# Loading v two tokens to a partition and putting it into key blocks with 0/1 matrices on TensorE

## The chip, the cores and the metric

The kernel runs on one core of a Trainium2 chip. The metric is the device time of one execution in microseconds (us). In the runs that compared the two kernels, the kernel before had a median of 204.88 us over four runs, 203.87 to 207.5. Medians are taken over all runs of a kernel, slow ones too. Ratios are the mean time of one kernel's fast runs over the mean of the other's fast runs of the same rounds, so they are not quite the ratios of the medians quoted. "Fast" and "slow" name two states that executions fall into: a run more than 1.5% above the fastest of its kernel in the same rounds is called slow, as the 207.5 us is.

## The reference, cut to what matters

```python
# q, k, v: [4, 8, 768, 64] float32; heads 0, 2, 6 are "retrieval" heads, the others "stream" heads
scores = q @ k.T / 8                      # causal; stream heads keep 4 sink tokens and a window of 64
a = softmax(scores)
attn = a @ v                              # -> x: [3072 tokens, 512]
# then a mixture of 8 experts, one expert for each token, tokens with x @ w_skip <= 0 skipped
y = gate * (relu(x @ w1[e]) @ w2[e]);  out = x + y
```

The change touches only how v reaches the product `a @ v`, and when some row buffers are zeroed for the expert layers.

## The kernel before

The attention loop works on 16 pairs of heads. Pass i computes the scores of pair i in chunks of 1,024 columns (two PSUM buffers, `pst`), takes their exp on ScalarE into `at`, and does the weighing, `at` times v, of pair i-1. It also transposes q and k of pair i+1. v is used from `va`, a buffer of six key blocks of 128 tokens with one token to a partition and a column of ones for the sum of the softmax. For stream heads there is also a shifted copy `vx`, in which the sink tokens are put into each block. Two `va` and two `vx` buffers alternate.

```python
vv = v.rearrange("b h (n p) d -> b p h n d", p=P)      # a run of memory is 64 floats, 256 B
...
def cast_v(i):
    va, vx = vab[i % 2], vxb[i % 2]
    nc.gpsimd.tensor_copy(va[:, :, :, :D], v32[i])      # float32 -> float16, straight into key blocks
    if i:
        nc.scalar.activation(xgs[i], xgs[0], ACT.Copy)  # zero one row buffer
    for hi, hh in enumerate(heads(i)[1]):
        if not IS_RETR[hh]:
            nc.gpsimd.tensor_copy(vx[:, hi], va[:, hi, :NQB - 1])
            nc.gpsimd.tensor_copy(vx[:N_SINK, hi], va[:N_SINK, hi, 0:1].to_broadcast(...))
...
for i in range(NPR + 2):                    # one pass
    cast_v(i); load_qk(i + 3); load_v(i + 2)
    step(0); transpose(i + 1, "q"); step(1)             # step: scores and exp of one chunk
    weigh(i - 1, 0)
    step(2); transpose(i + 1, "k"); cast_qk(i + 2)
    # some passes: gate_weight, left  (routing work on VectorE)
    step(3); gate_transpose(i - 2); weigh(i - 1, 1); step(4)
    # some passes: place, right       (routing work)
    gate_logits(i - 2)
```

GpSimd and VectorE run their instructions in the order in which they were written. In the kernel before, for example, one `gx` starts on GpSimd at 110.76 us though its numerators were done at 104.32, behind a cast that waited 10.09 us for v and the copies after it; and VectorE takes up sums at 60.95 us that TensorE had finished at 59.12, behind an operation of 2.15 us.

The softmax here doesn't subtract the row's maximum and nothing guards it: scores larger than these inputs give would overflow.

## Time and profile before

| | before |
|---|---|
| time, median | 204.88 us |
| profiled span, TensorE clock | 201.9 us, 0.958 |
| TensorE busy | 163.2 us, 81% |
| ordinary pass of the loop | 6.05 us |
| last exp of the gate (end of attention, start of the last routing) | 121.28 us |

Two waits of TensorE matter. In the list of waits the columns are: who waited and for whom, us in total, how often, the longest.

```profile
PE pst L578 <- ACT at L606: 9.3, 14, 0.8
PE opsa L626 <- POOL va L505: 4.0, 1, 4.0
```

The first is the regular wait for a score buffer, about 0.7 us in a pass: it is slack that TensorE has after the second chunk. The second is the one wait for v, of pair 14, near the end of the loop; behind it, from 109.82 to 113.59 us, the granted clock was 0.55. A good measure is the start of ScalarE's copy `qT` of each pair: the difference of two neighbours is the length of one pass.

### The profile page before, as it was taken

The numbers are of one execution on the slowest core, as the hardware profiler recorded it, in microseconds if no ns is written. First come the engines' busy times: TensorE is split into PE (matmuls) and PEld (weight loads), VectorE is DVE, ScalarE is ACT, GpSimd is POOL, SyncE is SP. The second block draws the span as 40 slices with busy tenths as digits, with TensorE's granted clock in tenths as the row PEclk, the third lists the DMA queues.
The fourth block names the chain that finished last, engine by engine and source line by source line (L and its number), as shares of the span: only waits on it lengthen the run. The fifth ranks groups of instructions, "written<-read, shape, count | busy, mean of one in ns | idle before, by whom it ended". The sixth has DMA issues, their size and how long they took to land.

```text
span 201.9 us, 4741 instructions
## 1 busy us (share of the span) xinstructions
PE 163.2 (81%) x1896; PEld 119.3 (59%) x1896; DVE 109.5 (54%) x254; ACT 113.0 (56%) x164; POOL 119.3 (59%) x179
## 2 busy tenths in 40 slices
PE   0487999889888898888982757978999999999920
PEld 0366666676666676666852443378678678665700
DVE  5323666636899668997650678253444534534020
ACT  5998888897688977888891420035143144130400
POOL 7585499687387693788403901687858575133311
PEclk9999999999999999999998795999999999999985
DMA  5999699999899999999999899479999999999501
GB/s 173 295 345 287 169 174 238 316 327 318 236 245 201 301 343 296 342 266 214 215 275 232 204 234 174 103 181 246 232 239 233 239 245 233 235 245 248 165 14 63
DMA packets 47856, 47.12 MB, mean 233 GB/s; under 512 B 28484, under 2 KB 43588, under 8 KB 46802
## 3 DMA queue, kind: packets, MB, share of 16 engines
q0 software_dynamic: 6976, 21.56, 50.3%
q1 hardware_dynamic: 40850, 25.17, 44.3%
q8 instruction: 17, 0.28, 0.6%
q14 instruction: 13, 0.11, 0.2%
HBM read 56.64 MB, written 10.49 MB: 333 GB/s over the span
## 4 chain that ended last, share of the span: by engine, by line
ACT 27%; DMA 26%; PE 23%; issue 8%; DVE 7%; POOL 6%; POOLq 1%; SPq 0%; ACTq 0%; DVEq 0%
ACT at L606 15%; DMA out_dram<-xg,idx_s 14%; DMA vf<-in_v_dram 10%; PE pst L578 5%; ACT xg L507 4%; PE pst L588 4%; PE hps L971 4%; ACT qT L526 4%; ACT gxT L675 3%; PE opsa L626 3%; POOL out_dram L1001 2%; PE pst L595 2%; PE yps L991 2%; POOL xg L935 2%; DMA xg<-out_dram,idx_s 1%
## 5 line engine op out<-in xcount | busy, mean ns | idle before, releaser
L606 ACT ACTIVATE at<-pst 128x1024 f16<-128x1024 f32 (+2 forms) x76 | 61.3, 836 | 17.2 <-PE pst L600 13.3
L978 ACT ACTIVATE ht<-hps 128x512 f16<-128x512 f32 x32 | 19.1, 598 | 49.4 <-PE hps L971 49.4
L588 PE MATMUL pst<-qT,kz 128*128 128x128 f16 (+2 forms) x288 | 35.8, 242 | 2.5 <-ACT qT L526 2.1
L588 PEld LDWEIGHTS <-kz 128*128 128x128 f16 x288 | 24.1, 100 | 21.9 <-issue 12.8
L535 DVE COPY kz<-tps 64x768 f16<-64x768 f16 x28 | 26.6, 950 | 9.7 <-PE tps L518 9.3
L971 PE MATMUL hps<-xT,w 128*128 128x256 f16 x256 | 29.2, 273 | 1.2 <-DVE xT L961 1.2
L971 PEld LDWEIGHTS <-w 128*128 128x128 f16 x256 | 27.9, 113 | 2.8 <-issue 1.5
L578 PE MATMUL pst<-smask,ident 128*128 128x512 f16 (+1 forms) x60 | 22.3, 372 | 8.7 <-ACT at L606 8.7
L991 PE MATMUL yps<-w,ht 128*128 128x512 f16 x128 | 28.8, 379 | 0.0
L1001 POOL DMA_INDIRECT out_dram<-xg,idx_s x16 | 16.4, 1022 | 18.5 <-issue 8.5
L649 POOL CAST gx<-xh 128x768 f16<-128x768 f32 x15 | 12.4, 828 | 19.3 <-DVE xh L641 14.5
L999 DVE SCALAR_TENSOR_TENSOR xg<-yps,gsl,xg 128x512 f32<-128x512 f32 x16 | 12.0, 750 | 20.4 <-PE yps L991 20.3
L626 PE MATMUL opsa<-va,at 128*128 128x65 f16 x372 | 19.8, 196 | 4.0 <-POOL va L505 4.0
L935 POOL DMA_INDIRECT xg<-out_dram,idx_s x16 | 16.8, 1047 | 8.6 <-issue 4.3
L626 PEld LDWEIGHTS <-at 128*128 128x128 f16 x472 | 17.9, 99 | 5.4 <-issue 4.2
L505 POOL CAST va<-vf 128x768 f16<-128x768 f32 x16 | 14.0, 876 | 11.2 <-DMA vf<-in_v_dram 11.1
L637 DVE RECIPROCAL rec<-opsa 128x6 f32<-128x6 f32 x32 | 6.2, 194 | 26.3 <-PE opsa L626 25.9
L991 PEld LDWEIGHTS <-ht 128*128 128x128 f16 x128 | 12.3, 98 | 13.5
L641 DVE TENSOR_TENSOR xh<-opsa,rec 128x384 f32<-128x384 f32 x32 | 17.8, 556 | 1.3
L499 POOL CAST qin<-qf 128x768 f16<-128x768 f32 x16 | 13.1, 818 | 3.3 <-DMA qf<-in_q_dram 3.3
L499 POOL CAST kin<-kf 128x768 f16<-128x768 f32 x16 | 13.1, 822 | 1.0 <-DMA kf<-in_k_dram 0.8
L518 PE MATMUL tps<-ident,qin 128*128 128x128 f16 x96 | 8.7, 231 | 5.9 <-POOL qin L499 5.9
(117 smaller groups left out, 260.7 us busy)
## 6 DMA issues: line engine op xcount, KB each, us to landing
w<-in_moe_w_dram POOLq DMA_DIRECT2D x14, 1024.0 KB, 10.7
qf<-in_q_dram SPq DMA_DIRECT2D x16, 384.0 KB, 6.3
kf<-in_k_dram SPq DMA_DIRECT2D x16, 384.0 KB, 6.0
vf<-in_v_dram SPq DMA_DIRECT2D x32, 192.0 KB, 6.0
out_dram<-xh SPq DMA_DIRECT2D x7, 768.0 KB, 6.8
w<-in_moe_w_dram POOLq DMA_DIRECT2D x4, 512.0 KB, 12.4
out_dram<-xh SPq DMA_DIRECT2D x2, 384.0 KB, 5.2
xg<-out_dram,idx_s POOLq DMA_INDIRECT x16, 7.2
```

The lines of the kernel that those rows point to most:

```text
L499: nc.gpsimd.tensor_copy(h16, qk32[name, i].rearrange("p h n d -> p n h d"))
L535: nc.vector.tensor_copy(to, ti[r])
L578: nc.tensor.matmul(pst[:, bank - c0:bank - c0 + mw], C.ident, rmask.unsqueeze(1).to_broadcast([P, mw // P, P]) if retr else smask[:, bank: ...
L588: nc.tensor.matmul(pst[:, cols], kz[:, j * P:(j + 1) * P], qT[i][:, qb * P:(qb + n) * P], start=mw <= 0, stop=mw <= 0 or last)
L606: nc.scalar.activation(ats[i][:, b0:b0 + cn], pst[:, :cn], ACT.Exp, scale=SCALE)
L626: nc.tensor.matmul(opsa[:, qb, :], ats[i][:, b0 + c:b0 + c + P], vb, start=(n == 0), stop=(n == len(plan) - 1))
L641: nc.vector.tensor_mul(xhs[i // 2][:, :, 2 * (i % 2) + hi, :], opsa[:, :, :D], rec.to_broadcast([P, NQB, D]))
L935: ins = nc.gpsimd.indirect_dma_start(out=xgs[t], out_offset=None, in_=out[:, :], in_offset=bass.IndirectOffsetOnAxis(ap=idx_s[:, t:t + 1], ...
L971: nc.tensor.matmul(hps[:, fi, :], wts[e, 0][:, s].rearrange("p (t c r) -> p t r c", c=P, r=WR)[:, fs // WR, fs % WR], xTs[e][:, s, :], sta ...
L978: nc.scalar.activation(ht[:, 2 * f2:2 * f2 + 2], hps, ACT.Relu)
L991: nc.tensor.matmul(ypss[s2], hts[e][:, fs, s2 * P:(s2 + 1) * P], wts[e, 1][:, fs, :], start=(fs == 0), stop=(fs == FS - 1))
L1001: ins = nc.gpsimd.indirect_dma_start(out=out[:, :], out_offset=bass.IndirectOffsetOnAxis(ap=idx_s[:, t:t + 1], axis=0), in_=xgs[t], in_off ...
```

## The change

The intent: v in runs of 512 B halves the number of its packets (q1 28,562 in all, instead of 40,850). Two tokens then lie side by side on a partition, which is not the order that the key blocks need, so four matmuls with 0/1 matrices (`pick`) bring them into place through PSUM. In return, eleven of the fifteen zeroings move to the routing.

```diff
-    vv = v.rearrange("b h (n p) d -> b p h n d", p=P)
+    vv = v.rearrange("b h (m p n) d -> b p h m (n d)", p=P, n=2)
...
-  tr_ps bufs=2, ov_ps bufs=2          # PSUM: transposes, sums of attention
+  tr_ps bufs=3, ov_ps bufs=1
...
+        pick = ac_pool.tile([P, 2, 2, P], FP16, name="pick")      # zeros, then:
+                nc.vector.tensor_copy(pick[:, half, n, n::2], C.ident[:, half * D:(half + 1) * D])
...
         def cast_v(i):
-            nc.gpsimd.tensor_copy(va[:, :, :, :D], v32[i])
-            if i:
-                nc.scalar.activation(xgs[i], xgs[0], ACT.Copy)
+            v16[i] = qk_in_pool.tile([P, 2, NQB // 2, 2, D], FP16, tag="vin", name="vin")
+            nc.gpsimd.tensor_copy(v16[i]..., v32[i])
+            zero(i)                                  # passes 3, 7, 11, 15 only
+        def order_v(i):
+            for half in range(2):
+                vps = tr_psum.tile([P, 2, NQB // 2, D], FP32, tag="tps", name="vps")
+                for n in range(2):
+                    nc.tensor.matmul(vps, pick[:, half, n], v16[i][:, :, :, n], start=n == 0, stop=n == 1)
+                to = va[:, :, half::2, :D]
+                if half == 0:
+                    nc.scalar.activation(to, vps, ACT.Copy)
+                else:
+                    nc.vector.tensor_copy(to, vps)
+            shift_v(i)                               # the two GpSimd copies into vx, as before
...
                 # end of the pass, behind place and right:
+                if i < NPR:
+                    order_v(i)
...
+            for t in range(5, NT):                   # in the routing, after the loop
+                nc.scalar.activation(xgs[t], xgs[0], ACT.Copy)
```

(The last pair's second head also takes its PSUM tile from the score buffers; the cut leaves that out.)

More of the change, by code (lines that the diff above doesn't have):

```diff
@@ L415 @@
          tc.tile_pool(name="st_ps", bufs=2, space=bass.MemoryType.PSUM) as st_psum, \
-         tc.tile_pool(name="tr_ps", bufs=2, space=bass.MemoryType.PSUM) as tr_psum, \
+         tc.tile_pool(name="tr_ps", bufs=3, space=bass.MemoryType.PSUM) as tr_psum, \
          tc.tile_pool(name="at", bufs=2) as at_pool, \
-         tc.tile_pool(name="ov_ps", bufs=2, space=bass.MemoryType.PSUM) as ov_psum, \
+         tc.tile_pool(name="ov_ps", bufs=1, space=bass.MemoryType.PSUM) as ov_psum, \
          tc.tile_pool(name="oo", bufs=3) as o_pool, \
@@ L438 @@
         nc.vector.memset(xgs[0], 0.0)
+        pick = ac_pool.tile([P, 2, 2, P], FP16, name="pick")
+        nc.vector.memset(pick, 0.0)
+        for half in range(2):
+            for n in range(2):
+                nc.vector.tensor_copy(
+                    pick[:, half, n, n::2],
+                    C.ident[:, half * D:(half + 1) * D])
         NPR = B * H // 2
-        qk32, v32, qk16, qT, ats, xhs, x16s, xTs = ({} for _ in range(8))
+        qk32, v32, v16, qk16, qT, ats, xhs, x16s, xTs = ({} for _ in range(9))
         gpss = {}
@@ L489, in load_v @@
             b, hs = heads(i)
-            vf = ld_pool.tile([P, 2, NQB, D], FP32, tag="vf", name="vf")
+            vf = ld_pool.tile([P, 2, NQB // 2, 2 * D], FP32, tag="vf",
+                              name="vf")
             for hi, hh in enumerate(hs):
@@ L503, in cast_v, with zero, shift_v @@
         def cast_v(i):
-            va, vx = vab[i % 2], vxb[i % 2]
-            nc.gpsimd.tensor_copy(va[:, :, :, :D], v32[i])
-            if i:
-                nc.scalar.activation(xgs[i], xgs[0], ACT.Copy)
+            v16[i] = qk_in_pool.tile([P, 2, NQB // 2, 2, D], FP16, tag="vin",
+                                     name="vin")
+            nc.gpsimd.tensor_copy(
+                v16[i].rearrange("p h m n d -> p h m (n d)"), v32[i])
+            zero(i)
+        def order_v(i):
+            va, vx = vab[i % 2], vxb[i % 2]
+            for half in range(2):
+                vps = tr_psum.tile([P, 2, NQB // 2, D], FP32, tag="tps",
+                                   name="vps")
+                for n in range(2):
+                    nc.tensor.matmul(vps, pick[:, half, n],
+                                     v16[i][:, :, :, n], start=n == 0,
+                                     stop=n == 1)
+                to = va[:, :, half::2, :D]
[4 more added lines that the diff above has]
+            shift_v(i)
+        def zero(i):
+            if i % 4 == 3:
+                nc.scalar.activation(xgs[(i + 1) // 4], xgs[0], ACT.Copy)
+        def shift_v(i):
+            va, vx = vab[i % 2], vxb[i % 2]
             for hi, hh in enumerate(heads(i)[1]):
@@ L622, in weigh @@
                                      vx[:, hi, qb - 1]))
-            opsa = ov_psum.tile([P, NQB, D + 1], FP32, tag="opsa",
-                                name="opsa")
+            if i == NPR - 1 and hi == 1:
+                last_ps = st_psum.tile([P, CH], FP32, tag="pst", name="opsl")
+                opsa = last_ps[:, :NQB * (D + 1)].rearrange(
+                    "p (n d) -> p n d", n=NQB)
+            else:
+                opsa = ov_psum.tile([P, NQB, D + 1], FP32, tag="opsa",
+                                    name="opsa")
             for n, (qb, c, vb) in enumerate(plan):
```

## The prediction

> **What bounds the kernel now.** I read the page first, then the timeline engine by engine for one ordinary pass of the attention loop and for its end, then the DMA issues. The kernel has an attention loop over 16 pairs of heads (to about 115 us), a routing stretch (to 132 us) and the expert layers (to 193 us).
>
> ```profile
> PE 163.2 (81%) x1896; PEld 119.3 (59%) x1896; DVE 109.5 (54%) x254; ACT 113.0 (56%) x164; POOL 119.3 (59%) x179
> ...
> q0 software_dynamic: 6976, 21.56, 50.3%
> q1 hardware_dynamic: 40850, 25.17, 44.3%
> ```
>
> DMA looks nearly full throughout, but v's landing time (a median of 6.0 us in the list of DMA issues) is far shorter than the prefetch distance of v (two passes, 12 us), so for most of the loop nobody waits for it. The timeline of an ordinary pass shows who does (ScalarE, then TensorE):
>
> ```profile
> 58.36 1.02 ACT L606 ACTIVATE at<-pst 128x1024 f16<-128x1024 f32 x1 [0.66 <-PE pst L600]
> 59.28 0.80 ACT L675 ACTIVATE gxT<-xtp 128x768 f16<-128x768 f16 x1
> 59.97 1.57 ACT L606 ACTIVATE at<-pst 128x384 f16<-128x384 f32 x2
> 61.44 0.81 ACT L526 ACTIVATE qT<-tps 128x768 f16<-128x768 f16 x1
> 62.13 1.63 ACT L606 ACTIVATE at<-pst 128x1024 f16<-128x1024 f32 x2
> 64.41 1.02 ACT L606 ACTIVATE at<-pst 128x1024 f16<-128x1024 f32 x1 [0.66 <-PE pst L600]
> ```
> ```profile
> 60.04 0.38 PE L588 MATMUL pst<-qT,kz 128*128 128x128 f16 x3
> ...
> 63.21 0.38 PE L578 MATMUL pst<-smask,ident 128*128 128x512 f16 x1 [0.74 <-ACT at L606]
> ```
>
> The period is 64.41 - 58.36 = 6.05 us. ScalarE idles 0.66 us in it, TensorE 0.74 us, both at the same place: with two score buffers, TensorE fills the fourth chunk (1.2 us) only when the second chunk's exp has freed its buffer. Everywhere else the two alternate. One point matters: the next pass's first chunk leaves TensorE at 60.42 us (60.04 + 0.38) and its exp starts at about 60.5, so there the slack is 0.1 us.
>
> Near the end a transfer does bind:
>
> ```profile
> 98.29 0.56 POOL L382 DMA_DIRECT2D w<-in_moe_w_dram  x1
> 108.94 0.83 POOL L505 CAST va<-vf 128x768 f16<-128x768 f32 x1 [10.09 <-DMA vf<-in_v_dram]
> ```
> ```profile
> 105.51 0.28 PE L595 MATMUL pst<-qT,kz 128*64 128x128 f16 x2
> 109.82 1.26 PE L626 MATMUL opsa<-va,at 128*128 128x65 f16 x21 [4.03 <-POOL va L505]
> ```
>
> v of pair 14 lands late: the queue issuing it was blocked for 10.47 us while 1 MB weight loads went out. TensorE stands for 4.03 us and then runs slowly: from 109.82 to 113.59 it does work that takes 2.4 us elsewhere, some 1.35 us more. So v's small transfers cost about 5.4 us, in this one place.
>
> [...] v now goes in runs of 64 floats, 256 B: 32 x 768 = 24,576 of the 40,850 packets of q1[...]. [...] (from 90 to 109 us q0 held 78% and q1 24%). [...] the trace's 512-column matmul at 57.16 us is followed at 57.37, 0.21 us[...]. [...] the trace has 492 ns for that exp, about 0.42 us net where instructions overlap.
>
> **The change part by part.**
>
> Loads: two tokens to a partition make runs of 512 B, 12,288 packets instead of 24,576. In the late stretch q1 had to pass one output store (768 packets) and v of pair 14 (1,536); now 768 + 768, two thirds. v lands about 5 us earlier after issue, and each pass also gets longer. I expect the wait to go: -4.0 and -1.35 us.
>
> Zeroing: nothing. The built order of ScalarE is the same in both programs: ten of the fifteen zero copies first, then qT, four more, and one in the first pass. The scheduler hoists the eleven copies written in the routing, because nothing holds them back. So the 8.1 us of these copies stay where they are, and ScalarE gets no relief in the loop.
>
> Reordering: 4 matmuls of 384 columns per pair, [...]0.65 us of TensorE, one ScalarE copy (0.42 us) and one VectorE copy (estimated 0.5 us, from 0.56 us for the 128x384 multiply from PSUM). They stand between the last chunk of a pass and the first chunk of the next, the place with 0.1 us of slack. The chunk leaves TensorE at 60.42 + 0.65 = 61.07, its exp begins 0.55 to 0.62 us later, and the rest of the period follows it. ScalarE's copy (60.5 to 60.9) fits before that. In the first two passes TensorE waits there anyway (0.1 us each); passes 2, 3, 4, 7, 8, 11, 12 and 14 pay about 0.62; passes 5, 9 and 13, where the gate logits already wait 0.25 us for ScalarE, about 0.45; passes 6 and 10 about 0.6. Sum 0.2 + 5.0 + 1.4 + 1.2 = 7.8 us.
>
> VectorE order: in the built order the VectorE half of the copy stands behind the routing work of its pass. In pass 7:
>
> ```profile
> 58.77 2.15 DVE L807 TENSOR_TENSOR Lall<-iota,posi 128x768 f16<-128x768 f16 x1
> 60.95 0.20 DVE L637 RECIPROCAL rec<-opsa 128x6 f32<-128x6 f32 x1
> 61.18 0.56 DVE L641 TENSOR_TENSOR xh<-opsa,rec 128x384 f32<-128x384 f32 x1
> 61.65 0.25 DVE L815 TENSOR_TENSOR oht<-iota,posi 128x96 f16<-128x96 f16 x1
> 61.93 1.10 DVE L819 TENSOR_TENSOR Rall<-oht,val 128x384 f16<-128x384 f16 x1
> 62.96 0.19 DVE L824 TENSOR_REDUCE ohn<-oh 128x8 f32<-128x48 f16 x1
> 63.18 0.56 DVE L825 TENSOR_TENSOR acc<-acc,ohn 128x8 f16<-128x8 f16 x1
> ```
>
> So va is whole at about 63.7 + 0.5 = 64.2 us, while TensorE wants it at 61.03 + 0.65 = 61.7: 2.5 us of wait, 0.74 of it slack, about 1.65 left. Pass 11 gives 1.35 by the same reckoning, passes 6 and 10 (behind the placing, then two GpSimd copies of 0.45 us) about 0.75 each: 4.5 us at most. The durations there depend on what GpSimd does at the time, so I count half, 2.2 us.
>
> Tail: the last pair's weighing now needs matmuls, evictions, the routing's VectorE work and GpSimd's shifted copies first: about 1.5 us.
>
> Buffers: the third transpose buffer removes a wait of 0.56 us in passes 6 and 10, but there v's first tile waits for VectorE's k copies, so I count none. The single output buffer is normally read out within 0.8 us, long before its next use.
>
> Sum: 7.8 + 2.2 + 1.5 - 5.4 = +6.1 us; 204.4 + 6.1 = 210.5 us.
>
> **The rivals.**
>
> A: DMA is the bound, and halving v's packets gives more than one wait back. For it: the DMA row at 9 nearly throughout. Against: before the end GpSimd waited for v only once, 1.0 us at 69 us, and nobody behind it stood still. It would give 196 to 201 us.
>
> B: the reordering hides in TensorE's and ScalarE's idle time. For it: both idle about 0.7 us a pass, as much as the change adds. Against: that idle time lies after the second chunk's exp, and the work is put before the first chunk. With it hidden only the wait removed and the tail count: about 200.5 us.
>
> C: every wait I found is real: all 4.5 us of VectorE order, 213 us. For it: the built order. Against: the pass gets longer too and VectorE, 54% busy, may catch up.
>
> D: the wait for v of pair 14 stays, because weights still hold the engines and the reordering needs v some 2 us earlier than the weighing did. The need is one end-of-pass later than the cast, though, and two longer passes lie between. It would add 3 to 5 us.
>
> **Range and chances.** C and my half of it span 210 to 213; B, or part of it, pulls towards 200 to 206, and whoever split the PSUM buffers so carefully may have seen a gain. I take 210.5 us with 203 to 215 for 8 in 10. The lines of 2% are 200.3 and 208.5: faster 0.10, same 0.30, slower 0.60.
>
> **What would show it.** Right: an ordinary pass of about 6.65 us instead of 6.05, with ScalarE waiting for TensorE before the first chunk's exp; the wait for v at pair 14 gone; TensorE waiting for va in the passes after 7 and 11; q1 with 28,562 packets; ScalarE still zeroing at the start. Wrong: a period still near 6.05 (then B), a shorter period everywhere (then A), or va's waits being absent, which takes the 2.2 us out.

## More of the kernel before

`weigh(i, 1)` ends with numerators on VectorE (`xh`) and a GpSimd copy for the gate (`gx`).

## The result, and the profile after

| | before | changed |
|---|---|---|
| time, median of four | 204.88 us | 214.8 us (213.56 to 216.28) |
| ratio of fast runs | | 1.0504, 95% interval 1.0407 to 1.0602 |
| profiled span, clock | 201.9 us, 0.958 | 212.1 us, 0.956 |
| ordinary pass | 6.05 us | 6.70 us |
| last exp of the gate | 121.28 us | 131.89 us |

The changed kernel is 5% slower. All of it is there by the end of attention: 131.89 - 121.28 = 10.6 us. From there to the end both kernels take about 80 us.

The queue row of the page (packets, MB, share of the engines' time) shows the load as intended, against 40,850 packets before:

```profile
q1 hardware_dynamic: 28562, 25.17, 37.7%
```

The ordinary pass on ScalarE (start, duration, engine, line, what; in brackets the idle time ahead of it and who ended it):

```profile
38.08 0.81 ACT L562 ACTIVATE qT<-tps 128x768 f16<-128x768 f16 x1
...
43.10 0.49 ACT L533 ACTIVATE va<-vps 128x384 f16<-128x384 f32 x1
43.86 1.02 ACT L642 ACTIVATE at<-pst 128x1024 f16<-128x1024 f32 x1 [0.28 <-PE pst L624]
44.78 0.81 ACT L562 ACTIVATE qT<-tps 128x768 f16<-128x768 f16 x1
```

The new copy `va<-vps` is there, and ScalarE now waits for TensorE right before the first chunk's exp. From `qT` to `qT` it is 6.70 us. In the passes with routing work TensorE also stands before the weighing:

```profile
60.44 0.19 PE L667 MATMUL opsa<-va,at 128*128 128x65 f16 x1 [1.15 <-DVE va L535]
61.54 0.19 PE L667 MATMUL opsa<-vx,at 128*128 128x65 f16 x1 [0.91 <-POOL vx L547]
...
62.42 0.38 PE L614 MATMUL pst<-smask,ident 128*128 128x512 f16 x1
```

First the VectorE half of the new copy is missing, then GpSimd's shifted copies. The list of waits sums them up; neither row was there before. Not all of these 10.3 us are lost, since part of them falls into slack that TensorE had anyway; experiment 6 measures what they cost:

```profile
PE opsa L667 <- DVE va L535: 6.8, 5, 1.6
...
PE opsa L667 <- POOL vx L547: 3.5, 4, 0.9
```

Near the end, GpSimd's cast of v of pair 14 waits for nothing any more. That of pair 15 still waits a little, and nobody behind it stands still for it:

```profile
111.75 0.82 POOL L517 CAST vin<-vf 128x768 f16<-128x768 f32 x1
120.79 1.60 POOL L517 CAST vin<-vf 128x768 f16<-128x768 f32 x1 [1.21 <-DMA vf<-in_v_dram]
```

And the last pair pays for the reordering once more:

```profile
125.38 0.21 PE L667 MATMUL opsa<-va,at 128*128 128x65 f16 x1 [1.59 <-DVE va L535]
126.49 0.22 PE L667 MATMUL opsa<-vx,at 128*128 128x65 f16 x1 [0.89 <-POOL vx L547]
```

**A side effect on VectorE.** In a routing pass one small operation grew. Before, and then in the changed kernel:

```profile
48.39 0.49 DVE L732 SCALAR_TENSOR_TENSOR eq<-sub,erev 128x48 f32<-128x48 f32 x1
```
```profile
51.25 2.65 DVE L773 SCALAR_TENSOR_TENSOR eq<-sub,erev 128x48 f32<-128x48 f32 x1
```

In the changed kernel GpSimd casts v, q and k back to back from 51.48 to 53.84 us, and the small operation ends just after them: 0.49 us became 2.65 us. (Even the 0.49 us stood beside a GpSimd copy; at 121.22 us in the kernel before, with no GpSimd cast or copy at that time, the operation took 0.21 us.) That the casts stretch it is what these three records suggest; no run here isolates it, or separates how much of the total it costs.

### The profile page after: what moved, and what is told of

The parts are those of the page before. It is cut to its first block, busy times and chain, and to the rows that moved or that the text cites. A ratio compares the mean times of both kernels' runs of the same rounds, so it can differ in the third digit from the quotient of the medians.

```text
span 212.1 us, 4981 instructions
## 1 busy us (share of the span) xinstructions
PE 174.3 (82%) x1960; PEld 125.7 (59%) x1960; DVE 120.5 (57%) x275; ACT 120.1 (57%) x180; POOL 119.5 (56%) x179
## 3 DMA queue, kind: packets, MB, share of 16 engines
q1 hardware_dynamic: 28562, 25.17, 37.7%
## 5 line engine op out<-in xcount | busy, mean ns | idle before, releaser
L624 PE MATMUL pst<-qT,kz 128*128 128x128 f16 (+2 forms) x288 | 35.2, 239 | 2.4 <-ACT qT L562 2.1
L1046 POOL DMA_INDIRECT out_dram<-xg,idx_s x16 | 17.0, 1061 | 19.0 <-issue 8.3
L667 PE MATMUL opsa<-va,at 128*128 128x65 f16 x366 | 20.6, 194 | 7.2 <-DVE va L535 6.8
L667 PEld LDWEIGHTS <-at 128*128 128x128 f16 x472 | 18.6, 99 | 13.3 <-issue 11.5
L614 PE MATMUL pst<-smask,ident 128*128 128x512 f16 (+1 forms) x60 | 21.7, 362 | 5.5 <-ACT at L642 5.3
L682 DVE TENSOR_TENSOR xh<-opsa,rec 128x384 f32<-128x384 f32 x31 | 17.3, 557 | 1.0
L528 PE MATMUL vps<-vin,pick 128*128 128x384 f16 x64 | 13.8, 328 | 1.6 <-ACT gxT L716 0.9
L517 POOL CAST vin<-vf 128x768 f16<-128x768 f32 x16 | 13.9, 867 | 1.2 <-DMA vf<-in_v_dram 1.2
L716 ACT ACTIVATE gxT<-xtp 128x768 f16<-128x768 f16 x15 | 12.1, 807 | 4.3 <-PE xtp L708 4.3
## 6 DMA issues: line engine op xcount, KB each, us to landing
w<-in_moe_w_dram POOLq DMA_DIRECT2D x14, 1024.0 KB, 10.6
w<-in_moe_w_dram POOLq DMA_DIRECT2D x4, 512.0 KB, 11.8
```

Of the source, the lines that this page charges most:

```text
L517: nc.gpsimd.tensor_copy(v16[i].rearrange("p h m n d -> p h m (n d)"), v32[i])
L614: nc.tensor.matmul(pst[:, bank - c0:bank - c0 + mw], C.ident, rmask.unsqueeze(1).to_broadcast([P, mw // P, P]) if retr else smask[:, bank: ...
L624: nc.tensor.matmul(pst[:, cols], kz[:, j * P:(j + 1) * P], qT[i][:, qb * P:(qb + n) * P], start=mw <= 0, stop=mw <= 0 or last)
L667: nc.tensor.matmul(opsa[:, qb, :], ats[i][:, b0 + c:b0 + c + P], vb, start=(n == 0), stop=(n == len(plan) - 1))
L682: nc.vector.tensor_mul(xhs[i // 2][:, :, 2 * (i % 2) + hi, :], opsa[:, :, :D], rec.to_broadcast([P, NQB, D]))
L1046: ins = nc.gpsimd.indirect_dma_start(out=out[:, :], out_offset=bass.IndirectOffsetOnAxis(ap=idx_s[:, t:t + 1], axis=0), in_=xgs[t], in_off ...
```

## The experiments

My theory after the result: the wide load is worth little; the reordering costs two things that add up, TensorE work at a place without slack and waits for its copies in the routing passes and at the end. The rival: there is a single cost, and the waits only stand in for it. Twelve kernels ran, with three rounds each and five for the last two.

**1 and 2: each half of the change alone.** The first is the kernel before with only the wide load; tokens and heads are misplaced, so its output is wrong. The second is the changed kernel with narrow loads and plain identities in place of `pick`; its output is correct.

```diff
# 1: before, plus
+    vv = v.rearrange("b h (m p n) d -> b p h m (n d)", p=P, n=2)
+            nc.gpsimd.tensor_copy(va..., v32[i]...)    # the cast goes straight to va, in the wrong order
# 2: changed, with
+    vv = v.rearrange("b h (n p) d -> b p h n d", p=P)
+            nc.vector.tensor_copy(pick[:, half, half], C.ident)
```

> The kernel before with only v's load changed to 512 B runs; tokens and the two heads of a pair land in wrong places, so the output is wrong on purpose (the routing still fits the capacity). No matmuls, no new copies. My theory (v's small packets cost one wait near the end and the slow clock behind it): about 5 us less than before, near 199 us, the ordinary pass still 6.05 us, GpSimd's 10.1 us wait for v of pair 14 gone. Rival A (DMA bounds the loop): the ordinary pass gets shorter too, 190 to 195 us. Rival D (weights keep the engines, the wait stays): within 1.5 us of before.

> The changed kernel with v loaded in 256 B runs again (the 0/1 matrices become identity and zero; result right, same matmuls, copies and order). My theory: the reordering makes the loop slower and the wide runs help only at the end, where the longer passes now leave more time for v; so 0 to 5 us more than the changed kernel, 214 to 220 us. If the loop's length comes from the transfers, it would differ from the changed kernel by more than 5 us, or be faster.

Measured: the wide load alone 203.31 us, ratio 0.9987 (0.9875 to 1.0099); the reordering alone 216.04 us, ratio 1.0574 (1.0458 to 1.069). The loss is the reordering's. The wide load missed its expectation. The trace says where its gain went:

```profile
98.83 0.84 POOL L506 CAST va<-vf 128x768 f16<-128x768 f32 x1
...
111.11 1.11 POOL L506 CAST va<-vf 128x768 f16<-128x768 f32 x1 [4.21 <-DMA vf<-in_v_dram]
```
```profile
112.27 0.27 PE L630 MATMUL opsa<-va,at 128*128 128x65 f16 x2 [2.33 <-POOL va L506]
```

Pair 14 no longer waits, but the load of pair 15 then lies behind the weight loads, and TensorE stands for it 2.33 us. The wait had moved one pair on. In the second kernel, with narrow loads, pair 14's cast did not wait for its load either: a slower loop, 6.71 us for an ordinary pass, gives the transfers more time. Only pair 15's cast stood still, for 2.81 us, and TensorE behind it for 0.91 us; the list of waits names TensorE as the cause, but by the list of DMA issues this pair's load took about 15.4 us to land, from its issue at 108.75 us, and that ends just before the cast.

**3 and 4: the same reordering at other places of the pass.** In the third kernel it stands ahead of the routing work at the end of the pass; in the fourth between the third chunk and the k transposes, where TensorE has its own slack. Both are correct.

```diff
# 3
+                if i < NPR:
+                    order_v(i)
                 if i > 5 and b < B - 1 and late == 1:
                     place(b)
# 4
                 step(2)
+                if i < NPR:
+                    order_v(i)
                 if i + 1 < NPR:
                     transpose(i + 1, "k")
```

> The changed kernel with v's reordering placed ahead of the routing's placing and one-hot work in its pass, so that VectorE's half of the copy no longer stands behind that work; nothing else moved. Theory (waits for va and vx in the passes after 6, 7, 10, 11 and in the tail cost about 5 to 6 us, the term that I halved): 3.5 to 6 us less than the changed kernel, 208.5 to 211 us; ordinary passes still about 6.7 us. Rival (those waits only show up because TensorE is ahead there and are swallowed by ScalarE's own period): less than 1.5 us.

> The changed kernel with v's reordering placed between the third score chunk and the k transposes of its pass, where both TensorE and ScalarE idled about 0.7 us in the kernel before. Theory (what costs is the place without slack, not the work): the ordinary pass goes back to 6.05 to 6.2 us, va's waits vanish, total 199 to 203 us, faster than both kernels. Rival (the added work itself is too much for ScalarE or TensorE): pass of 6.5 us or more, total 208 us or more.

Measured: 212.98 us, ratio 1.0426 (1.0343 to 1.0509), and 219.69 us, ratio 1.0737 (1.0541 to 1.0933). Both missed. In the third, VectorE's copy came earlier, and another engine took its place:

```profile
61.79 0.19 PE L667 MATMUL opsa<-vx,at 128*128 128x65 f16 x1 [1.93 <-POOL vx L547]
```
```profile
59.29 0.83 POOL L690 CAST gx<-xh 128x768 f16<-128x768 f32 x1 [5.18 <-DVE xh L682]
...
60.75 0.47 POOL L546 COPY vx<-va 128x325 f16<-128x325 f16 x1
```

On GpSimd the shifted copies stand behind `gx`, and `gx` waits for VectorE's numerators. So moving one copy ahead gained only 1.8 us of the 3.5 to 6 expected, and since the intervals of the two ratios overlap, not even that is clear of the noise.

In the fourth, ordinary passes did return to 6.06 us (`qT` at 40.17 and 46.23 us), which confirms that the place made them long. But the routing passes grew, one to 11.2 us, because cast, reordering and shifted copies of the same pair now followed each other closely on engines that took them in the order written, and GpSimd's copies waited for `va`, 42.2 us in all:

```profile
POOL vx L546 <- ACT va L533: 27.9, 10, 4.5
POOL vx L546 <- DVE va L535: 14.3, 6, 4.7
```

**5: half the matmuls.** One matmul for each half instead of two; output wrong.

```diff
-                for n in range(2):
-                    nc.tensor.matmul(vps, pick[:, half, n], v16[i][:, :, :, n], ...)
+                nc.tensor.matmul(vps, C.ident, v16[i][:, :, :, 1 - half], start=True, stop=True)
```

> The changed kernel with one identity matmul for each half in place of two pick matmuls, so half the TensorE work of the reordering and everything else kept; heads and tokens are misplaced and the output is wrong on purpose. Theory (the TensorE work of the reordering stands at a place without slack): each ordinary pass shortens by 0.32 us (6.70 to about 6.4 us) and the total by 3 to 5 us, to 210 to 212 us, as the half-finished copies also come earlier. Rival (the copies to key blocks and the shifted copies set the length of the pass, not the matmuls): the pass stays near 6.7 us and the total falls by less than 1.5 us.

Measured: 213.75 us, ratio 1.0464 (1.0396 to 1.0533). The pass did what the theory said: 45.26 - 38.87 = 6.39 us, 0.31 less than 6.70. The total followed by only 1 us, where 3 to 5 were expected. The reason is visible in the same stretch as above:

```profile
60.91 0.19 PE L665 MATMUL opsa<-va,at 128*128 128x65 f16 x1 [1.30 <-DVE va L533]
62.02 0.19 PE L665 MATMUL opsa<-vx,at 128*128 128x65 f16 x1 [0.92 <-POOL vx L545]
...
63.38 0.63 PE L612 MATMUL pst<-smask,ident 128*128 128x512 f16 x1
```

The two waits stayed, and after them TensorE ran at the slow clock, in the records from 62.29 to 65.37 us: 0.63 us for a matmul that takes 0.38. This pass took 9.25 us with a mean granted clock of 0.82, against 7.85 us at 1.00 in the changed kernel, and the same happened again four passes later (9.23 us, 0.82). Stands like these were not always followed by it: 1.16 and 0.92 us, with a single short matmul between, were followed by the full clock in the changed kernel (the pass from 89.51 us, 7.87 us long, 1.00) and by the slow one in the eighth kernel (the pass from 87.39 us, 9.45 us long, 0.82). What decides between the two is not shown. So a pass with such waits lost another 1.4 to 1.6 us in these two kernels, and none in the changed kernel, where both such passes ran at 1.00. Whether this is what spreads the changed kernel's runs from 213.56 to 216.28 us is not shown, since only one execution of it was profiled.

**6: the reordering one pass ahead, at the same place.** Pass i now reorders v of pair i+1. The TensorE work and its place are the same; only the reader comes a pass later. Its output is correct.

```diff
-                    cast_v(i)   ...   load_v(i + 2)   ...   order_v(i)
+                    cast_v(i + 1)   ...   load_v(i + 3)   ...   order_v(i + 1)
```

> The changed kernel with the reordering one pass ahead: at the same place, the end of pass i, v of pair i+1 is reordered in place of v of pair i; v is cast one pass earlier; two va buffers as before. The TensorE work at the place without slack is the same, the reader of va and vx comes a whole pass later, so the waits for them (about 5 us in the trace) should all go. Theory (ordinary 0.65 us per pass and the waits are two separate terms that add): ordinary pass still 6.7 us, no wait for va or vx, total 5 us shorter, 208.5 to 211 us. Rival (the waits only hold the place of others: TensorE would then wait for VectorE's numerators, GpSimd's casts or v from the DMA queue instead): total 213 us or more; v of the last pairs is now needed a pass earlier, so the DMA wait could be back.

Measured: 208.62 us, ratio 1.0218 (1.0152 to 1.0283), with the ordinary pass still at 6.70 us. The waits for `va` and `vx` are gone from the weighing, and TensorE has its regular slack back even in the routing pass that stood before:

```profile
61.78 0.38 PE L614 MATMUL pst<-smask,ident 128*128 128x512 f16 x1 [0.85 <-ACT at L642]
```

This run tells the theories apart. Waits and TensorE work are two separate costs: the waits are 6.2 us of the median (5.8 us by the ratios, 5.89 us in the traces at the gate's last exp), the rest remains.

**7 and 9: one pass ahead and in mid pass.** Both use a third `va` buffer and one buffer for the cast v. The seventh casts v of pair i+1 at the start of pass i; the ninth casts it half a pass earlier, behind the casts of q and k and ahead of `gx`. Both are correct.

```diff
                 step(2)
+                    order_v(i + 1)          # 7 and 9
                     transpose(i + 1, "k")
                     cast_qk(i + 2)
+                    cast_v(i + 2)           # 9 only
...
+                    shift_v(i + 1)          # end of the pass, 7 and 9
```

> The reordering one pass ahead and in the middle of the pass (after the third chunk's scores, ahead of the k transposes), with a third va buffer, one buffer for the cast v, and the shifted copies left at the end of the pass. Theory: the TensorE work then lies where TensorE had slack of its own and no copy is waited for, so the ordinary pass is 6.05 to 6.15 us and the routing passes lose nothing: 200 to 205 us, at or just under the kernel before. Rival (the routing passes lose to the order of work on GpSimd and VectorE whatever the distance): routing passes stay over 7.5 us and the total is above 209 us.

> As the reordering one pass ahead in the middle of the pass, but v is cast half a pass before it is reordered, right after the casts of q and k and ahead of the copy for the gate, so that GpSimd does not hold it behind its wait for VectorE's numerators (that wait was 48 us in the run before, and TensorE waited 17.2 us for the cast v). Theory (place without slack, and the order of work on GpSimd, are what the reordering costs; both are now taken away): ordinary pass 6.05 to 6.15 us, no wait for the cast v, routing passes at most 8 us, total 198 to 205 us, at or below the kernel before. Rival (the mere work of the reordering on TensorE, ScalarE and VectorE lengthens the pass wherever it stands, or the single buffer for attention's sums does): passes of 6.5 us and more, total 208 us or more.

The seventh failed: 222.6 us, ratio 1.09 (1.0836 to 1.0964). Its waits name the cause. The cast stood behind `gx` on GpSimd, and the matmuls now needed it early in the pass:

```profile
PE vps L530 <- POOL vin L519: 17.2, 12, 2.5
```

The ninth changes only where the cast stands (and, with it, issues v's loads half a pass earlier; in the seventh a cast waited for its load only once, 1.8 us). It took 203.34 us, ratio 0.9924 (0.9773 to 1.0075): 19 us less than the seventh, and within its interval the same as the kernel before. The whole reordering is in it, and the ordinary pass is back:

```profile
31.11 0.81 ACT L563 ACTIVATE qT<-tps 128x768 f16<-128x768 f16 x1
...
33.29 0.52 ACT L535 ACTIVATE va<-vps 128x384 f16<-128x384 f32 x1
...
37.16 0.80 ACT L563 ACTIVATE qT<-tps 128x768 f16<-128x768 f16 x1
```

**8: the zeroing really held back.** In the changed kernel the eleven copies written in the routing are started at the beginning all the same, because nothing holds them back. Writing their source once more, late, does. Its output is correct.

```diff
+            nc.gpsimd.memset(xgs[0], 0.0)           # after the loop
             for t in range(5, NT):
                 nc.scalar.activation(xgs[t], xgs[0], ACT.Copy)
```

> The changed kernel with the source row of zeros written once more late on GpSimd, so that the eleven zero copies written in the routing really stay there (in the changed kernel as built they are started on ScalarE at the beginning). Theory: the copies at the start lie in time in which ScalarE waits for data anyway, and late they lie beside the routing's small operations: within 1 us of the changed kernel, 214 to 216 us. Rival (they delay the first passes on ScalarE): 2 to 4 us faster, with the first qT copies earlier.

Measured: 214.6 us, ratio 1.0495 (1.0398 to 1.0592), the same as the changed kernel. The first `qT` came at 5.87 instead of 8.83 us, as the rival had it, but of that only 1.5 us was left at the last exp of the gate (130.4 us) and 0.4 us in the span. Up to `qT` of pair 12 the lead was 2.1 us; then a pass at the slow clock (9.45 us at 0.82 instead of 7.87 at 1.00) and the next one together took 0.8 us of it.

**10: PSUM as before.** The ninth kernel with two transpose buffers and two for the sums of attention.

```diff
-  tr_ps bufs=3, ov_ps bufs=1
+  tr_ps bufs=2, ov_ps bufs=2
```

> The same with PSUM shared out as in the kernel before (two buffers for transposes, two for attention's sums). If the single buffer for attention's sums was what the routing passes waited for (3 to 4 us of waits for VectorE's numerators in the kernels with the reordering in mid pass), 2 to 4 us faster than the run before it; if three buffers for transposes are what the reordering needs, 3 us or more slower.

Measured: 215.39 us, ratio 1.0504 (1.0389 to 1.0619). The transposes now waited 11.8 us, 15 times, for VectorE's copy of `va` to free a buffer. So three transpose buffers and one for the sums beat two and two by some 12 us in that arrangement.

**11: the ninth kernel with narrow loads. 12: the kernel before, with v only loaded and cast a pass earlier** (three `va` and `vx` buffers, nothing of the change). Both are correct.

```diff
# 11: as in experiment 2, on kernel 9
# 12: before, with
-                    cast_v(i)   ...   load_v(i + 2)
+                    cast_v(i + 1)   ...   load_v(i + 3)
```

> The kernel of the ninth run (reordering one pass ahead in mid pass, v cast early) with v loaded in 256 B runs as before and brought into key blocks by plain identities, so the reordering is paid for and the wide load is not there. Theory (where the reordering costs nothing, the wide load is worth what it was worth alone, 1 to 2 us): 203.5 to 206 us, within 1.5 per cent of the ninth run's ratio of 0.992. Rival (the wide load now has its full worth of 4 us or more, because it is the DMA queue that the last pairs wait for): 207 us or more, ratio 1.01 or more.

> The kernel before with v loaded and cast one pass earlier (three buffers for va and vx) and nothing of the change: 256 B runs, no reordering. Theory (the 10 us wait for v of pair 14 is a matter of when its load is issued, ahead of the expert weights or behind, not of the size of its packets): GpSimd may still wait but TensorE no longer stands for v, and the time is 199 to 202 us, ratio 0.97 to 0.985. Rival (the wait only moves to v of the last pair, or to other work, as it did with the wide load alone): 203 to 205 us, ratio 0.99 to 1.0.

Measured: the eleventh 203.54 us, ratio 0.9954 (0.9882 to 1.0027); the twelfth 204.1 us over all six runs, three of them slow, ratio of the fast ones 0.9877 (0.9755 to 1.0). With and without the wide load, the ninth and eleventh kernels differ by 0.3%, less than their intervals. Together with experiments 1 and 2 (0.1% and 0.7%) the wide load was worth less than 1.5 us wherever it was measured, and nowhere more than the noise. The twelfth ended between its theory (0.97 to 0.985) and its rival (0.99 to 1.0): TensorE no longer stands for v, but the time fell less than expected.

In the twelfth kernel the wait for v at the end goes without any wide load. GpSimd still waits for the last v, but TensorE has a pass in hand:

```profile
104.65 0.82 POOL L505 CAST va<-vf 128x768 f16<-128x768 f32 x1 [3.73 <-DMA vf<-in_v_dram]
```

From the start of `qT` of pair 15 to the last exp of the gate it takes 117.84 - 101.83 = 16.01 us, against 121.28 - 99.79 = 21.49 before: 5.5 us. Of that 2.1 us are lost again in one pass (9.69 us instead of 7.61), where GpSimd waits 3.04 us for k, perhaps because k's load now stands beside an earlier v (not tested). So its lead over the kernel before, 1.2%, is at the edge of its interval. It beats the changed kernel clearly; it does not beat the kernel before by 2%.

It also shows that the ninth kernel does not get the reordering for nothing. The last exp of the gate comes at 117.84 us in the twelfth kernel, with v early and no reordering, at 120.82 us in the ninth and at 121.28 us in the kernel before. So some 3 us of the reordering remain in the ninth, in routing passes (8.06, 6.64 and 6.78 us, where the kernel before has 7.35 to 7.61, 6.05 and 6.06), in some of which TensorE waits 0.8 to 1.0 us for VectorE's numerators. What it gains by not waiting for v makes up for them.

Pass lengths, from `qT` to `qT`, in us:

| pass between the starts of qT | before | changed | 5, half the matmuls | 6, ahead, at the end | 9, ahead, mid pass |
|---|---|---|---|---|---|
| 5 to 6, ordinary | 6.06 | 6.70 | 6.39 | 6.71 | 6.06 |
| 8 to 9, behind the placing | 6.05 | 7.85 | 9.25 | 6.71 | 6.64 |
| 9 to 10, behind the rest of the routing work | 6.06 | 7.44 | 6.38 | 6.70 | 6.78 |
| 12 to 13, as 8 to 9 | 6.05 | 7.87 | 9.23 | 6.70 | 6.63 |
| 13 to 14, as 9 to 10 | 6.06 | 7.44 | 6.38 | 6.71 | 6.14 |
| 15 to the last exp of the gate | 21.49 | 19.45 | 19.14 | 16.66 | 16.55 |

## Why the prediction was right or wrong

The direction was right, and so was the mechanism of the reordering; the size was too small. Predicted was 210.5 us, +6.1; measured was 214.8 us, near the upper end of the range. The step that failed is the one on the waits for the copies, which the prediction counted at half; the tail and the passes around the routing work were mis-sized too, and the reason given for v's wait was wrong. In the traces the term by term account is +10.6 us at the last exp of the gate.

- **Zeroing, nothing: right.** Experiment 8 shows that even really moving it changes nothing that the total shows.
- **Ordinary passes, +7.8: right in mechanism, 1.7 us too small.** The step from 6.05 to 6.70 us is the predicted one, and the 6.39 us with half the matmuls shows that it is TensorE work at that place. From the first `qT` to the last, the passes grew by 12.65 us; taking out the 3.8 us of the next point leaves 8.9, and the pass after adds about 0.6: 9.5 us. In the kernel before, a long pass is followed by a short one, so I compare these in pairs. From 2 to 4 they took 1.38 us more, where I had about 0.7; from 6 to 8 and from 10 to 12 1.42 us more each, where I had 1.05; and the pass from 14 to 15 0.74 us, where I had 0.45. The 0.65 us of TensorE and the 0.42 us of ScalarE's copy in the prediction were my estimates, the second from the 492 ns of an exp of 128x384; in the changed kernel the four matmuls took 0.66 us from start to start (94.77 to 95.43) and the copy 0.51 us. In each of the three pairs the reordering waits for a transpose buffer (0.24 us in the first, 0.65 us in the others), and I had written "I count none" there:

```profile
PE vps L528 <- ACT gxT L716: 0.9, 3, 0.3
PE vps L528 <- DVE kz L571: 0.7, 2, 0.3
```

  In the ninth kernel, with the reordering in mid pass, these waits are gone, and the last two pairs are 0.69 us longer than before instead of 1.42.
- **The waits for va and vx in routing passes, +2.2: the step that failed.** I had worked out 4.5 us "at most" and then wrote "I count half", because VectorE might catch up. The four passes in the table took 3.8 us more than in experiment 6, where these waits are gone (v is also loaded and cast a pass earlier there): 1.14 + 0.74 + 1.17 + 0.73. Behind the rest of the routing work (passes 7 and 11) the half was about right: of the 1.65 and 1.35 us worked out, 0.73 us was left each time. VectorE's `Lall`, which had taken 2.15 us while GpSimd was casting, started as the casts ended and took less than half of that:

```profile
64.66 0.96 DVE L848 TENSOR_TENSOR Lall<-iota,posi 128x768 f16<-128x768 f16 x1
```

  Behind the placing (passes 6 and 10) it was wrong: I had 0.75 us each and counted half, and 1.15 us was paid. TensorE stood twice there, 1.15 us for VectorE's half of the copy and then 0.91 us more for the shifted copies that GpSimd makes from it, and its slack of about 0.74 us covers only a part.
- **The tail, +1.5: a mis-sized term of the same kind.** The stretch after the last `qT` changed by 19.45 - 21.49 = -2.0 us. With -5.5 for v (next point) and about +0.6 for one ordinary reordering, 2.9 us are left for the tail. Experiment 6 takes 2.8 us out of that stretch, and the trace has waits of 1.59 and 0.89 us there, again one behind the other.
- **The wait for v of pair 14, -5.4: right in size, but not for the reason given, so the number was partly luck.** It is gone in the changed kernel, and experiment 12 measures its worth as 5.5 us. But it is not the wide load that removes it: the load alone only passed it on to pair 15 and gained no more than 1.4 us at the last exp, and the slow loop with narrow loads kept only 0.91 us of it. Nor did v land sooner for its wide runs: with the load alone q1's share of the engines' time fell from 44.3% to 39.8%, but v's median landing time was 7.1 us, against 6.0 before. What removes the wait is time between issue and use. That two thirds of the packets would bring v about 5 us earlier was my estimate; why v landed slowly beside the weights (a median of 13.7 us from 90 to 109 us, where q0 held 78% and q1 24%) no run tests.
- **The rivals.** A (DMA is the bound) is refuted by experiment 1: fewer packets, the same time. B (the reordering hides) is refuted for the place chosen; at another place it is true of the ordinary passes and not of the routing passes: experiment 9. C (every wait is real) was the nearest, at 213 us. D (the wait stays) did not come.

The account: +9.5 + 3.8 + 2.9 - 5.5 = +10.7 us (10.6 before rounding), where 7.8 + 2.2 + 1.5 - 5.4 = 6.1 had been predicted. Of the 4.5 us missing, about 3.0 are waits for the copies that the reordering ends in (1.6 in the routing passes, 1.4 in the tail), and 1.7 lie in the passes around the routing work. Experiment 6 took the waits for the copies away together and gained 6.2 us. What stays open: why those passes cost more than the ordinary ones (the waits for a transpose buffer and the stretched VectorE operation are candidates, and no run isolates them), and how much of the spread of the changed kernel comes from the granted clock (0.941 to 0.957 in its four runs).

## What to carry to other kernels

When work is added to a software pipeline, ask two things of it apart: does it stand where its engine has slack, and how far behind it is its reader? Here one pass more of distance was worth 6 us, another place in the pass and a cast ahead of a waiting copy on GpSimd another 5, and nothing of the work itself had to be taken away. That made the reordering cheap, not free, and a kernel without it was at least as fast. The single long wait for a transfer was here a matter of when it was issued; before making packets larger, try issuing the transfer earlier. And when waits are read from the built order, follow the chain of engines to its end: one wait shrank to half when an operation ahead of it ran beside no casts (`Lall`, 0.96 us instead of 2.15), and another grew by half because a second engine's copies stood behind it.
